# Zeros for the idle fill, an early exponential, other homes for the words of w_v, and a new order table

## The chip, the cores and the metric

The kernel runs on one core of a Trainium2 chip. The metric is the time of one execution on the device, in microseconds (us); the profile shows one such execution, engine by engine. PE is the matrix engine (TensorE), DVE the vector engine, ACT the scalar engine, POOL GpSimd, SP the engine that issues most of the transfers.

## The reference

Three stages on 4 x 576 tokens of width 512: attention with a window of 64 keys, a gated feed-forward block, and a convolution gate with two products. Cut to what is computed:

```python
scores = matmul(q, k.T) / sqrt(64)                      # 4 batches, 8 heads, 576 x 576
mask = (rel >= 0) & (rel < 64)                          # rel = query position - key position
attn = softmax(where(mask, scores, -1e9))
x = matmul(attn, v)                                     # -> 4 x 576 x 512
x_prev = x shifted by one token (zeros at the start)
xk = mu_k * x + (1 - mu_k) * x_prev;  xr = mu_r * x + (1 - mu_r) * x_prev
h = relu(xk @ w_k) ** 2                                 # 512 -> 1024
x = sigmoid(xr @ w_r) * (h @ w_v)                       # r and v, each 512 wide
gate = sigmoid(sum over 5 taps of conv_w[t] * x shifted by t)
out = (gate * (x @ w_val)) @ w_out
```

q, k, v are float32, the weights arrive as 64-bit numbers.

## The kernel before

The 2304 tokens are cut in five blocks: block 0 with 256 tokens, blocks 1 to 4 with 512. For each block there are four attention units, one for each pair of heads, numbered 0 to 19, so that units 0 to 3 belong to block 0 and units 4 to 7 to block 1. A unit is a chain over the engines: `ldqk` and `ldv` (SP issues the loads of q, k and v), `qk` (scores on PE), `top` (row maximum on DVE), `exp` (ACT), `eps`, `rec`, `norm` (the division, DVE), `tp0` and `tp` (transposes of the two heads on PE), `pt` (copies out of PSUM), `pv` (PE), `x` (copy into `xT`). A block's `mix` steps then form xk and xr (`a` on ACT or DVE, `xm` on DVE).

Every weight piece takes a chain of its own. `ld` loads the 64-bit words, `g` (ACT) and `t`, `s` (DVE) make float32 "words" of them, and `hi` and `lo` split these in two fp32r tiles, so that blocks 1 to 4 multiply hi*hi + hi*lo + lo*hi. Activations are split likewise (`xhi`, `xlo`). Block 0 starts earlier: its products `r`, `h` and `v` use the float32 words themselves (line 577), the later blocks the split tiles (line 554). Block 1 cannot start before its `xlo` are written, and these lie in the tile `x` (tag "x"), which before the change is the same memory as the tile `words`. `wide_x` is the step that hands it over: it waits until all ten pieces have given up their words. After block 4 the last stage runs (`val`, `out`), in which POOL issues six accumulating transfers into `gate`.

What runs when is not decided on the chip. Every step has a number in the table SLOT; the steps are sorted by it, and each engine runs its instructions in that order. A step that waits holds everything behind it on its engine, the transfers that SP and ACT issue among them. The costs in `Plan` decide one thing in the program: how many idle passes `fill` puts ahead of a PE step that would wait (line 994). These are products of the identity tile into a spare PSUM tile, meant to keep PE active. Exponentials and sigmoids lie in different tables of ACT; an ACT_TABLE_LOAD stands where they alternate.

Of the kernel before, what the change touches and what calls it, by code (L numbers as in the profile page):

```python
# [8 lines left out]
F32 = mybir.dt.float32  # L9
# [11 lines left out]
P = 128  # L21
# [19 lines left out]
    'first': '5',  # L41
    'cap': '6',
    'ident': '10',
    'low': '11',
    'ldmu': '1',
    'ldc': '14',
    'omu': '27',
    'pg': '59',
    'wc0': '89 26 96',
    'wc': '99',  # L50
    'first_x': '4',
    'ldqk': '0 8 7 16 18 40 105 107 164 209 231 247 301 310 338 401 398 425 445 479',
    'ldv': '20 22 44 46 67 102 211 219 250 280 297 312 355 382 427 441 485 483 540 537',
    'qk': '12 15 25 34 42 76 157 201 226 243 285 304 336 347 393 422 440 476 491 502',
    'top': '13 19 31 41 49 123 165 208 249 264 317 331 346 390 413 435 457 487 498 533',
    'exp': '17 23 43 50 64 141 183 215 260 268 319 334 349 405 420 447 461 489 503 553',
    'eps': 'v24 v35 p51 p58 p75 p152 p192 p223 p267 p276 p325 v343 p358 p410 p430 v450 p466 p508 v509 p556',
    'rec': '29 39 55 72 83 163 204 236 271 281 327 351 359 412 434 458 471 510 525 557',
    'norm': '30 45 62 78 97 184 214 241 277 294 328 353 361 417 438 463 472 511 529 560',
    'tp0': '32 53 68 86 106 194 225 246 283 300 335 360 391 421 448 467 490 515 542 573',  # L60
    'pt': 'a38 v48 a56 v63 a74 a77 a91 a94 a117 a169 a213 a212 a229 a235 a251 a257 a286 a291 a302 a306 a341 '
        'a342 a369 v373 a394 v404 a432 a429 v451 a454 a470 a477 v492 a499 a518 v532 a544 v551 v588 a592',
    'tp': '37 60 71 92 130 207 230 255 289 303 337 368 397 424 452 475 494 522 548 589',
    'pv': '52 66 82 98 185 216 239 273 293 308 350 377 407 436 460 478 512 534 564 600',
    'x': 'v54 v69 a85 a101 a193 a228 a252 a284 a298 a333 a364 v384 v418 a443 a473 a482 a520 v538 a586 a624',
    'mask': '237 258 290 322 340 386 408 428 455 480 496 531',
    'edge': '242 262 295 326 345 389 411 433',
    'a': 'a79 v104 a110 a120 a240 a253 a288 a292 v352 v356 v431 a439 v493 a497 v572 a575 v595 a633 a638 a649',
    'xm': '84 111 114 126 261 272 299 311 383 375 459 446 505 501 578 582 620 640 648 652',
    'xlo': '90 115 119 131 282 287 309 318 419 423 488 474 571 568 584 593 636 646 661 677',  # L70
    'carry': '133 132 278 316 385 464 507 585',
    'r': '93 116 109 124 100 125 112 121 313 320 400 409 554 550 558 567 625 631 639 635 716 728 723 736',
    'sig': '127 128 134 137 329 330 414 437 562 566 576 579 641 642 645 647 725 738 739 750',
    'h': '135 142 144 153 139 146 148 155 168 187 177 188 162 182 174 197 339 354 324 332 363 370 381 387 514 '
        '495 504 517 524 530 536 543 602 603 608 605 614 621 618 609 678 686 682 673 695 700 705 710',
    'relu': 'a158 a167 a160 a166 a191 a195 a198 a203 v348 a362 v344 a366 a374 a378 v388 a396 a516 a519 v513 v523 '
        'a539 a546 a545 v549 v604 a606 v610 v611 a619 v627 a622 a623 v694 a697 a687 a690 a711 a712 v713 a717',
    'sbuf': '170 171 199 205',
    'slo': 'a172 a180 v202 a206 371 379 402 406 535 541 561 563 615 617 637 634 708 709 737 726',
    'v': '210 270 218 234 256 265 248 263 449 469 426 453 415 462 442 481 596 598 591 597 574 583 569 580 650 '  # L80
        '662 658 667 653 672 643 657 749 759 776 789 742 766 755 783',
    'x2': '307 314 323 321 484 465 468 506 601 599 590 594 668 675 674 670 788 794 781 790',
    'xhi': 'a275 a279 v305 a315 a416 v392 a486 a456 a570 a565 v581 a587 v626 a644 v651 v671',
    'cut': '259 296 357 444 500 577',
    'shi': '365 372 380 399 521 527 547 552 607 613 628 629 698 699 719 721',
    'sq': 'a367 a376 v395 a403 v526 a528 a559 a555 v612 v616 v630 a632 a701 v702 a729 a724',
    'staging': '3',
    'w_r ld': '9 21',
    'w_r g': '33 61',
    'w_r t': '36 57',  # L90
    'w_r s': '65 70',
    'w_r hi': 'a113 v80',
    'w_r lo': '145 143',
    'w_k ld': '47 28 122 87',
    'w_k g': '95 81 154 151',
    'w_k t': '108 73 147 140',
    'w_k s': '118 88 159 156',
    'w_k hi': 'v138 a103 v173 v181',
    'w_k lo': '150 129 189 217',
    'w_v ld': '149 136 179 190',  # L100
# [949 lines left out]
```

## Time and profile before

| what | value |
| --- | --- |
| median of 3 runs | 435.81 us (435.57 to 435.96) |
| time of the profiled execution | 435.19 us |
| span of the profiled execution | 433.4 us |
| PE busy | 418.4 us, 97% of the span |
| DVE, ACT busy | 319.8 us, 254.9 us |
| PE's share of the chain that ended last | 90% |

The span runs from the first instruction to the last; 1.8 us of the execution lie around it. A row of the timeline gives start, duration, engine, line, operation, output<-inputs, how many instructions were merged into it, and in brackets how long the engine was idle ahead of it and what ended that.

### The profile page before, as it was taken

The page shows a single profiled execution, that of the slowest core. Times are in us where ns is not written, and L with a number is a line of the kernel's source. Part 1 is how long each engine was busy: PE and PEld are TensorE (multiplying, and loading weights), DVE is VectorE, ACT ScalarE, POOL GpSimd, SP SyncE. Part 2 cuts the span into 40 slices and gives each one's busy share as a digit, 9 for nine tenths or more (in the row PEclk, how much of TensorE's full clock was granted, in tenths as well). Part 3 has the DMA queues.
Part 4 walks back from the last instruction along what each step waited for, and adds up shares of the span by engine and source line. Part 5 has one row for each costly group of instructions (what it writes and reads, how often), then busy time and mean ns, then how long its engine had stood idle before and what let it go on. Part 6 is the DMA issues. An engine that isn't in the chain of part 4 may idle for free.

```text
span 433.4 us, 7910 instructions
## 1 busy us (share of the span) xinstructions
PE 418.4 (97%) x3200; PEld 359.9 (83%) x3200; DVE 319.8 (74%) x443; ACT 254.9 (59%) x581; POOL 23.8 (5%) x66
## 2 busy tenths in 40 slices
PE   5799999899999999999999999999999999999996
PEld 4588787788888888888888888888888999999996
DVE  3999999956976884747314581589996999999960
ACT  3989899697498574394102553045442787785431
POOL 1002202000000100001000000000000000010000
PEclk9999999999999999999999999999999999999999
DMA  7997753722315152100110005220224545543112
GB/s 257 405 332 313 274 170 108 250 68 63 109 47 203 48 174 74 51 0 2 48 50 0 2 0 206 98 97 2 97 88 143 194 98 165 163 117 103 56 56 109
DMA packets 16692, 52.44 MB, mean 121 GB/s; under 512 B 1936, under 2 KB 2704, under 8 KB 15120
## 3 DMA queue, kind: packets, MB, share of 16 engines
q1 hardware_dynamic: 14784, 42.10, 28.0%
q0 software_dynamic: 864, 3.54, 4.1%
q10 hardware_dynamic: 1008, 6.30, 3.8%
q8 instruction: 25, 0.41, 0.4%
q14 instruction: 11, 0.09, 0.1%
HBM read 38.95 MB, written 9.44 MB: 112 GB/s over the span
## 4 chain that ended last, share of the span: by engine, by line
PE 90%; DMA 4%; DVE 2%; ACT 2%; POOL 1%; issue 1%; ACTq 0%; POOLq 0%; DVEq 0%
PE h L554 20%; PE v L554 20%; PE out L554 12%; PE r L554 10%; PE at L467 4%; PE qk L393 4%; PE at L455 3%; PE v L577 3%; PE val3m L785 3%; PE val2m L785 3%; PE val1m L785 3%; PE val0m L785 2%; DMA qk<-qk 2%; DMA words<-w_v 2%; PE r L577 2%; PE h L577 2%
## 5 line engine op out<-in xcount | busy, mean ns | idle before, releaser
L554 PE MATMUL h<-x,wk 128*128 128x512 f32 x384 | 91.1, 393 | 0.0
L554 PEld LDWEIGHTS h<-x,wk 128*128 128x128 f32 x384 | 71.1, 188 | 14.9 <-issue 0.2
L554 PE MATMUL v<-sh,wv 128*128 128x512 f32 x256 | 82.0, 393 | 0.0
L554 PEld LDWEIGHTS v<-sh,wv 128*128 128x128 f32 x256 | 48.0, 188 | 10.1 <-issue 0.2
L554 PE MATMUL v<-sl,wv 128*128 128x512 f32 x128 | 49.8, 389 | 0.0
L603 ACT ACTIVATE rk<-h 128x512 f32<-128x512 f32 (+1 forms) x28 | 14.4, 544 | 56.3 <-PE h L554 47.5
L554 PE MATMUL r<-x,wr 128*128 128x512 f32 x192 | 45.3, 392 | 0.0
L554 PEld LDWEIGHTS r<-x,wr 128*128 128x128 f32 x192 | 35.7, 188 | 7.5
L741 DVE SCALAR_TENSOR_TENSOR gate<-xb,wc,gate 128x576 f32<-128x576 f32 x52 | 40.4, 813 | 0.1
L437 ACT ACTIVATE s<-s,m 128x128 f32<-128x128 f32 x96 | 37.2, 389 | 4.2 <-DVE m L426 4.1
L654 DVE TENSOR_TENSOR sgs<-v,sgs 128x512 f32<-128x512 f32 (+1 forms) x20 | 12.5, 633 | 24.2 <-PE v L554 24.2
L554 PEld LDWEIGHTS v<-sl,wv 128*128 128x128 f32 x128 | 24.1, 188 | 4.7
L460 ACT ACTIVATE pt<-at 128x512 f32<-128x512 f32 (+1 forms) x31 | 16.8, 562 | 18.0 <-PE at L455 17.9
L554 PE MATMUL out<-g0h,wr 128*128 128x288 f32 x128 | 27.0, 295 | 0.0
L554 PE MATMUL out<-g1h,wr 128*128 128x288 f32 x128 | 27.0, 295 | 0.0
L467 PEld LDWEIGHTS at<-pt,vt 128*64 128x64 f32 x576 | 19.4, 140 | 8.3 <-issue 3.3
L455 PE MATMUL at<-ident,s 128*128 128x128 f32 x144 | 23.0, 279 | 2.6 <-DVE s L447 1.5
L467 PE MATMUL at<-pt,vt 128*64 128x64 f32 x576 | 22.5, 228 | 2.0 <-ACT pt L460 0.8
L605 DVE TENSOR_SCALAR rk<-h 128x512 f32<-128x512 f32 x12 | 8.2, 687 | 22.0 <-PE h L554 21.9
L455 PEld LDWEIGHTS at<-ident,s 128*128 128x128 f32 x144 | 16.6, 140 | 8.1 <-issue 1.4
L518 DVE SCALAR_TENSOR_TENSOR xm<-xT,omu,xm 128x512 f32<-128x512 f32 x32 | 22.4, 742 | 0.7 <-POOL xT L524 0.7
L632 DVE TENSOR_TENSOR sl<-rk,sh 128x1024 fp32r<-128x1024 f32 x16 | 19.4, 1221 | 4.7 <-ACT rk L630 4.6
(139 smaller groups left out, 810.6 us busy)
## 6 DMA issues: line engine op xcount, KB each, us to landing
qk<-qk SPq DMA_DIRECT2D x16, 544.0 KB, 4.3
vt<-vh SPq DMA_DIRECT2D x16, 512.0 KB, 4.6
xb<-x2d SPq DMA_DIRECT2D x4, 1152.0 KB, 6.8
out_t<-st SPq DMA_DIRECT2D x15, 288.0 KB, 2.1
x2d<-sgs SPq DMA_DIRECT2D x16, 256.0 KB, 2.0
gate<-tt POOLq DMA_DIRECT2D x6, 576.0 KB, 5.0
words<-w_r SPq DMA_DIRECT2D x2, 1024.0 KB, 7.1
words<-w_k ACTq DMA_DIRECT2D x2, 1024.0 KB, 7.9
```

Source lines behind the costliest of these rows:

```text
L393: PE.matmul(a["ps"][heads[c % 2], h, c // 2 * P:c // 2 * P + P], lhsT=a["q"][heads[h], c * W:(c + 1) * W], rhs=a["k"][heads[h], c * W:c * ...
L437: ACT.activation(out=s, in_=scores()[:, c // n2, c % n2, :] if by_pe else s, func=AF.Exp, scale=D ** -0.5 if by_pe else 1.0, bias=l(0)[:, ...
L455: PE.transpose(a["tp", h][:, c * P:(c + 1) * P], a["s"][:, h * n2 + c, :], ident)
L460: ("act", p_ns(n), lambda h=h: ACT.activation(out=a["pt"][:, h, :n], in_=a["tp", h][:, :n], func=AF.Copy)),
L467: PE.matmul(a["o"][heads[h], c * W:(c + 1) * W], lhsT=a["v"][:, c, heads[h]], rhs=a["pt"][:, h, c * W:(c + 1) * W], start=True, stop=True)
L518: V.scalar_tensor_tensor(out=m, in0=xT[:, f, :n], scalar=omu[:, c:c + 1], in1=m, op0=ALU.mult, op1=ALU.add)
L554: PE.matmul(ps, lhsT=a, rhs=b[:, kt, :], start=(kt == 0 and i == 0), stop=(kt == nk - 1 and i == 2))
L577: PE.matmul(Ps[key][:, :n], lhsT=ws(kt), rhs=x()[:, kt, :], start=kt == 0, stop=kt == nk - 1)
L603: ACT.activation(out=o, in_=ps, func=AF.Relu)
L632: lambda E: E.tensor_tensor(out=Ss[t][1][:, f, :n], in0=rk(), in1=f32(Ss[t][0][:, f, :n]), op=ALU.subtract))
L741: V.scalar_tensor_tensor(out=g, in0=src, scalar=c, in1=g, op0=ALU.mult, op1=ALU.add)
L785: PE.matmul(z[bank][:, j, :HS], lhsT=lhs, rhs=rhs, start=new and kt == 0 and e == 0, stop=kt == 1 and e == 2, skip_group_check=not new)
```

## The change

Six things are changed.

- **Fill.** The idle passes of PE read a tile of zeros, `warm`, the first 128 columns of `sgs`, which POOL writes as its first own instruction. They no longer need the identity.
- **An exponential of one column.** A new step `table` runs one on ACT, into the first column of the second quarter of `sgs`.
- **DMA scratch.** The scratch for POOL's transfers is 2048 bytes per partition.
- **Words of w_v.** The space that this frees holds a new tile `early` (three pieces of 1024 words). The words of w_v lie there and in the second half of `rk`; those of w_r and w_k stay in `words`. `wide_x` waits for six pieces instead of ten, and for two `s`. In block 1 the odd pairs of `relu` wait for `lo` of w_v's last piece and for one `v` of block 0.
- **Loads** of the later pieces are issued from ACT, once the `s` of an earlier piece is done (before: its `hi`).
- **Costs and SLOT** are new.

```diff
 SLOT = {
-    'first': '5',
-    'cap': '6',
+    'first': '33',
+    'cap': '5',
+    'warm': '2',
+    'table': '462',
...
-    START, LAND = 700, 1100
-    RAMP, SLOW = 3500, 1.6
-    WAIT, PASS = 700, 480
+    BEGIN, START, LAND = 740, 700, 1270
+    RAMP, STALL = 3500, 1300
+    WAIT, PASS = 700, 600
...
+    early = const.tile([P, 3 * 1024], F32, name="early")
...
+    warm = sgs[:, 0, :P]
+    op("warm", "pool", 110, [], lambda: G.memset(warm, 0.0))
+    op("table", "act", 100, ["warm"], lambda: ACT.activation(out=sgs[:, 1, :1], in_=warm[:, :1], func=AF.Exp), table="exp")
...
+        E = ACT if queue == "act" else DMA
+        op((key, "ld"), queue, 60 if queue == "act" else 420, [*after, *([(prev, "s")] if prev else [])],
+           lambda: E.dma_start(out=raw_of(), in_=w_dram[key[1]].bitcast(I32)), moves=2.55 * n)
...
-                    Rk[t, p] = rks[:, p % 2]
+                    Rk[t, p] = rks[:, p % 2] if t else rks[:, 0, :, p % 2 * TA:(p % 2 + 1) * TA]
...
-            plan.any(("relu", t, 2 * p + i), [("h", t, 2 * p + i), *back("slo", 2), *([("relu", t, 2 * p)] if i else [])],
+            plan.any(("relu", t, 2 * p + i), [("h", t, 2 * p + i), *back("slo", 2), *([("relu", t, 2 * p)] if i else []),
+                      *([(("w_v", 3), "lo"), ("v", 0, 3)] if t == 1 and p % 2 else [])],
...
-        Q["raw"] = [a.bitcast(I32) for a in (w[:, 0], w[:, 1], xr[:, 1], sr[:, 1])]
-        Q["sw"] = [w[:, 2 + i, j * 1024:(j + 1) * 1024] for i in range(2) for j in range(2)]
+        Q["raw"] = [a.bitcast(I32) for a in (xr[:, 1], sr[:, 1], w[:, 0], w[:, 1])]
+        s = [w[:, 2 + i, j * 1024:(j + 1) * 1024] for i in range(2) for j in range(2)]
+        Q["sw"] = s + s[:2] + [early[:, j * 1024:(j + 1) * 1024] for j in range(3)] + [rks[:, 1].rearrange("p i n -> p (i n)")]
...
-    op("wide_x", "none", 0, [(p[0], "lo") for p in pieces] + [u for p in pieces for u in users[p[0]]], wide_x)
+    op("wide_x", "none", 0, [(p[0], "lo") for p in pieces[:6]] + [u for p in pieces[:6] for u in users[p[0]]]
+       + [(p[0], "s") for p in pieces[6:8]], wide_x)
...
-            PE.matmul(idle["ps"][:, 0, :P], lhsT=ident, rhs=ident, start=True, stop=True)
+            PE.matmul(idle["ps"][:, 0, :P], lhsT=warm, rhs=warm, start=True, stop=True)
...
-    nc = bacc.Bacc("TRN2", target_bir_lowering=False, num_devices=1)
+    nc = bacc.Bacc("TRN2", target_bir_lowering=False, num_devices=1, dynamic_dma_scratch_size=2048)
```

What the new table does to the order is shown at three places. The first is the queue of SP near the program's start, before the change; the names qk, vt, w_r and w_k are those of the tiles and weights, and the qk rows with 1088 columns belong to units 4 and 5.

```order
L323 DMA words<-w_r 128x2048
L288 DMA cw<-conv 128x40
L366 DMA qk_133<-qk 128x576
L366 DMA qk_189<-qk 128x1088
L372 DMA vt_193<-vh 128x512
L323 DMA words<-w_r 128x2048
L372 DMA vt_193<-vh 128x512
L323 DMA s_117<-w_k 128x2048
L366 DMA qk_255<-qk 128x1088
```

The same place of the same queue after the change.

```order
L329 DMA s_114<-w_r 128x2048
L372 DMA qk_184<-qk 128x1088
L378 DMA vt_188<-vh 128x512 x2
L329 DMA x_113<-w_r 128x2048
L372 DMA qk_261<-qk 128x1088
L378 DMA vt_286<-vh 128x512 x2
L329 DMA words<-w_k 128x2048 x2
L372 DMA qk_311<-qk 128x1088
```

Unit 5's load, the second row with 1088 columns, moved from behind the first piece of w_k to ahead of it, and `conv` is gone from here. Once w_r's `s` is done, ACT issues the third piece of w_k beside this queue.

The second place is DVE ahead of block 1, before the change. L329 is the `lo` of a weight piece, L408 a unit's mask, L426 its `top`, L447 its `norm`, L518 `xm`, and L541 the `xlo` of block 1.

```order
L329 TENSOR_TENSOR wv_77<-words,wv_76 128x8x128
L426 TENSOR_REDUCE m_827<-s_770 128x8
L329 TENSOR_TENSOR wv_77<-words,wv_76 128x8x128
L408 SCALAR_TENSOR_TENSOR s_847<-qk_795,cap 128x1024
L518 SCALAR_TENSOR_TENSOR xm<-xT,omu,xm 128x512 x2
L426 TENSOR_REDUCE m_866<-s_847 128x8
L329 TENSOR_TENSOR wv_77<-words,wv_76 128x8x128 x2
L445 RECIPROCAL m_827<-m_827 128x8
L518 SCALAR_TENSOR_TENSOR xm<-xT,omu,xm 128x512 x2
L447 TENSOR_TENSOR s_770<-s_770,m_827 128x1024
L445 RECIPROCAL m_866<-m_866 128x8
L541 TENSOR_TENSOR x<-xm,x 128x1024 x2
```

DVE ahead of block 1 after the change; L547 is `xlo`, L335 `lo`, L662 the `x2` of block 0.

```order
L547 TENSOR_TENSOR x<-xm,x 128x1024
L313 TENSOR_SCALAR x_113<-x_113 128x1024
L547 TENSOR_TENSOR x<-xm,x 128x1024
L315 SCALAR_TENSOR_TENSOR early<-early,x_113 128x1024
L432 TENSOR_REDUCE m_926<-s_849 128x8
L524 SCALAR_TENSOR_TENSOR xm<-xT,omu,xm 128x512 x2
L545 CAST x<-xm 128x1024
L547 TENSOR_TENSOR x<-xm,x 128x1024
...
L662 TENSOR_TENSOR sgs<-v_0_842,sgs 128x256
L335 TENSOR_TENSOR wv_78<-rk,wv_77 128x8x128
```

The four `lo` of w_v moved from ahead of block 1's `xlo` to behind them. Ahead of the `xlo` that block 1's first product needs DVE now has four `lo`, one mask, one `norm` and one cast less. PE has one attention unit less there (16 rows of `qk`, 8 transposes, 16 rows of `pv`), and block 1 begins with `h` instead of `r`.

The third place is ACT in block 1, where the exponential of the new step (L294) stands; L443 are the exponentials of the units, L466 and L480 copies.

```order
L443 ACTIVATE s_1549,m_1557<-s_1549,m_1557 128x128 x8
L466 ACTIVATE pt_1624<-at_1625 128x512
L480 ACTIVATE xT<-at_1588 128x512
L511 ACTIVATE xm<-xT,sm 128x512 x2
L466 ACTIVATE pt_1624<-at_1656 128x512
L294 ACTIVATE sgs<-sgs 128x1
L480 ACTIVATE xT<-at_1680 128x512
```

It is row 125 of ACT's 281 in this list. The first table load stands where it stood, ahead of unit 0's exponentials, as row 2. The new step writes, at that place, one column of `sgs` in which a sigmoid of block 1 lies until the product with `v` has read it.

At the very start PE has four idle instructions (three before), then `qk` of units 0 and 1 with no fill between them (before: two), then five.

## Rows read from the trace of the kernel before

**Rows 1.** The page: the span.

```profile
span 433.4 us, 7910 instructions
```

**Rows 2.** Windows: busy us, (instructions) of PE, PEld, DVE, ACT, POOL; PEclk, DMA share, GB/s.

```profile
0.00:10.00 10.00, 5.50 (x64) 4.56 (x66) 2.48 (x9) 2.87 (x10) 1.95 (x11) 1.00 0.76 246
10.00:20.00 10.00, 7.29 (x130) 5.01 (x131) 9.86 (x24) 9.91 (x46) 0.57 (x3) 1.00 1.01 400
...
20.00:22.00 2.00, 1.65 (x34) 1.41 (x32) 2.00 (x6) 2.00 (x5) 0.26 (x1) 0.56 1.03 429
...
350.00:400.00 50.00, 50.00 (x377) 50.00 (x377) 48.56 (x69) 36.34 (x55) 4.05 (x6) 1.00 0.49 131
```

**Rows 3.** Timeline of PE, its first instructions.

```profile
3.09 1.65 PE L994 MATMUL idle<-ident 128*128 128x128 f32 x6 [3.09 <-POOL ident masks.py:199]
...
4.90 1.16 PE L393 MATMUL qk<-qk 64*64 64x128 f32 x16
5.99 0.98 PE L994 MATMUL idle<-ident 128*128 128x128 f32 x4
...
7.04 0.65 PE L393 MATMUL qk<-qk 64*64 64x128 f32 x16
```

**Rows 4.** Transfers issued in the first 0.9 us: KB, us to landing.

```profile
qk<-qk SPq DMA_DIRECT2D x1, 288.0 KB, 3.0
```

**Rows 5.** Timeline of POOL, DVE and ACT near the start.

```profile
2.47 0.20 POOL masks.py:197 MEMSET ident<- 128x128 f32 x1
3.07 0.23 DVE L283 CAST one<-ident 128x128 bf16<-128x128 f32 x1 [0.32 <-POOL ident masks.py:199]
7.12 1.28 ACT L437 ACT_TABLE_LOAD   x1 [7.12 <-DVE m L429]
15.81 1.18 ACT L301 ACTIVATE words<-words 128x1024 f32<-128x1024 f32 x1
```

**Rows 6.** The chain that ended last, around unit 5's load: start us, us, what.

```profile
12.36 8.19 DMA qk<-qk
```

**Rows 7.** Timeline of PE from unit 5's scores to block 0's first product.

```profile
19.81 0.41 PE L385 MATMUL qk<-low,one 64*64 64x512 bf16 x4 [0.24 <-ACT s L437]
...
20.59 1.99 PE L393 MATMUL qk<-qk 64*64 64x128 f32 x32 [0.35 <-DMA qk<-qk]
22.51 1.12 PE L467 MATMUL at<-pt,vt 128*64 128x64 f32 x16
23.56 0.99 PE L455 MATMUL at<-ident,s 128*128 128x128 f32 x4
24.39 1.03 PE L577 MATMUL r<-x,words 128*128 128x256 f32 x4
25.35 0.69 PE L467 MATMUL at<-pt,vt 128*64 128x64 f32 x16
```

**Rows 8.** Timeline of PE ahead of block 1.

```profile
74.32 0.63 PE L455 MATMUL at<-ident,s 128*128 128x128 f32 x4 [0.66 <-DVE s L447]
74.88 1.10 PE L393 MATMUL qk<-qk 64*64 64x128 f32 x32
...
77.46 1.15 PE L467 MATMUL at<-pt,vt 128*64 128x64 f32 x30 [0.64 <-ACT pt L460]
79.11 1.06 PE L455 MATMUL at<-ident,s 128*128 128x128 f32 x8 [0.50 <-DVE s L447]
...
82.22 2.11 PE L554 MATMUL r<-x,wr 128*128 128x512 f32 x8
```

**Rows 9.** Timeline of DVE ahead of block 1.

```profile
61.51 1.22 DVE L329 TENSOR_TENSOR wv<-words,wv 128x1024 fp32r<-128x1024 f32 x1
```

**Rows 10.** Tile gate on POOL: duration ns min/median/max, first and last start; issues by line.

```profile
L757 POOL DMA_DIRECT2D gate<-tt x6: 840/844/1017, 344.7 to 387.6; - x6
...
gate<-tt POOLq DMA_DIRECT2D x6, 576.0 KB, 5.0
```

**Rows 11.** Transfers by line: a piece of w_k issued by ACT.

```profile
words<-w_k ACTq DMA_DIRECT2D x2, 1024.0 KB, 7.9
```

More of the change, by code (lines that the diff above doesn't have):

```diff
@@ L194, in run @@
             t = max((end[d] + hop[d] for d in ready), default=0)
-            t = max(t + (self.TO_PE if w[0] == "pe" and t else 0), free.get(w[0], 0) if w[0] != "none" else 0)
+            t = max(t + (self.TO_PE if w[0] == "pe" and t else 0), free.get(w[0], self.BEGIN))
             t += self.TABLE if tab and tab != table else 0
             table = tab or table
-            if w[0] == "pe" and self.fill and t - free.get("pe", 0) > self.WAIT:
-                self.fill(t, int((t - max(free.get("pe", 0), 1500) - 250) // self.PASS))
-            free[w[0]] = end[key] = t + w[1]
+            if w[0] == "pe" and self.fill and t - free.get("pe", self.BEGIN) > self.WAIT:
+                self.fill(t, int((t - max(free.get("pe", 0), 1100) - 250) // self.PASS))
+            end[key] = t + w[1]
+            if w[0] != "none":
+                free[w[0]] = end[key]
             hop[key] = self.HOP[w[0]]
             if moves:
-                link = max(link, end[key] + self.START) + moves * (self.SLOW if link < self.RAMP else 1)
+                new = max(link, end[key] + self.START) + moves
+                link = new + self.STALL * (link < self.RAMP <= new)
                 end[key] = link + self.LAND
@@ L307, in words, with weight @@
                                           op0=ALU.logical_shift_left, op1=ALU.bitwise_or))
[L309 removed]
+    def weight(key, w_dram, dst, nm, raw_of, s_of, prev=None, sprev=None, after=(), free=(), used=(), queue="dma"):
         nk = w_dram.shape[2] // nm
         n = nk * nm
[L316 to L323 removed]
+        raw = lambda: raw_of().rearrange("p (k m t) -> p k m t", k=nk, t=2)
+        s = lambda: s_of().rearrange("p (k m) -> p k m", k=nk)
+        E = ACT if queue == "act" else DMA
+        op((key, "ld"), queue, 60 if queue == "act" else 420, [*after, *([(prev, "s")] if prev else [])],
+           lambda: E.dma_start(out=raw_of(), in_=w_dram[key[1]].bitcast(I32)), moves=2.55 * n)
         words(key, n, raw, s, [(key, "ld")], [*used, *([(sprev, "lo")] if sprev else [])])
@@ L396, in qk @@
                               skip_group_check=by_pe)
-        op(("qk", u), "pe", 1040 * nc_ // 8 + 270 * by_pe, [("ldqk", u), *(["low"] if by_pe else []), *([] if t else ["idle"])], qk,
+        op(("qk", u), "pe", 1034 * nc_ // 8 + (208 if t == 0 else 241) * by_pe, [("ldqk", u), *(["low"] if by_pe else []), *([] if t else ["idle"])], qk,
            ring=("pq" if t else "p0", ("exp" if by_pe else "mask", u)))
@@ L429, in top @@
             V.tensor_scalar(out=l(0), in0=l(0), scalar1=D ** -0.5, scalar2=None, op0=ALU.mult)
-        op(("top", u), "dve", v_ns(n * 2) + 72 * by_pe, [("qk" if by_pe else "edge" if firsts else "mask", u), *back2("norm")], top)
+        op(("top", u), "dve", v_ns(n * 2) + 190 * by_pe, [("qk" if by_pe else "edge" if firsts else "mask", u), *back2("norm")], top)
         def exp():
@@ L456, in unit @@
         for h in range(2):
[L457 removed]
+            op(("tp", u) if h else ("tp0", u), "pe", 88 * n2 + 2, [("norm", u), "ident", *back("pv", 1), *([("tp0", u)] if h else [])], lambda h=h: tp(h),
                ring=("pa", ("pt", u, h)))
```

41 lines of the change are left out of this document (16 added, 25 removed), and 200 rows, old and new, of the table SLOT.

## The prediction

> **What bounds the kernel now.** The page comes first: the span is 433.4 us [rows 1], and by the table above PE is busy for 97% of it and makes nine tenths of the chain that ended last. The order table neither adds nor removes a product, so PE's useful work stays what it is. [...]
>
> The start: PE's first pass comes at 3.09, block 0's first product only at 24.39 [rows 3, 7]. In between, ACT and DVE are busy 9.91 and 9.86 of 10 us [rows 2]: they work through the exponentials and through the weights' words, and PE waits for them. So what starts these two engines earlier is worth its full length, until something else holds PE.
>
> The stretch from 19.8 to 24.4: unit 5's scores wait 0.24 us for an exponential and 0.35 for their own load, whose step in the chain is 8.19 us long [rows 6, 7]. [...]
>
> The stretch ahead of block 1: three waits of 0.66, 0.64 and 0.50 us, two for a `norm` on DVE and one for a copy on ACT [rows 8].
>
> Behind it the trace has no wait of PE until the last stage begins. That stage is PE-bound too, with PE busy for 50 of 50 us and DVE for 48.56 [rows 2].
>
> **The change part by part. The fill and the first scores (A).** Unit 0's load lands 3.0 us after its issue at 0.74, so at 3.75 [rows 4]. Its float32 scores started only at 4.90, because six idle passes, started at 3.09 when the identity was there, lay ahead. They ran until 6.06 at the low clock: 16 rows in 1.16 us, against 0.65 for unit 1 [rows 3]. After the change the fill waits for a memset of the size that takes 0.20 us [rows 5], issued at about 0.74, so I put the first pass at 1.0. Eight passes at 1.65/6 = 0.275 us end at 3.2. The mask operands are ready at 3.07 + 0.23 = 3.30 [rows 5], the load at 3.75, so the float32 part starts at about 3.8. Before, the clock rose between 5.99 (four passes in 0.98 us, still slow) and 7.04 (fast) [rows 3], so 2.9 to 3.95 after the first pass; the same lead from 1.0 gives 3.9 to 4.95. The scores then end between 3.8 + 0.65 = 4.45 and 3.8 + 1.16 = 4.96. I take 4.85, near the slow end, since most of the rise's interval lies behind 4.45. That is 1.2 us sooner than 6.06; bounds 1.1 and 1.6. The maximum, the table load and the exponentials follow as one chain, so all of it is passed on.
>
> **The early exponential (nothing).** The order puts the new step in block 1, as row 125 on ACT, and leaves the first table load ahead of unit 0's exponentials. So the load's 1.28 us [rows 5] stays on the path. The step itself is one column, less than a copy, on an engine with room there; without that cover it would cost one short ACT instruction.
>
> **Unit 5's load and the low clock (B).** In SP's queue one piece of w_k, 1024 KB, no longer lies ahead of unit 5's load. At the 400 GB/s of [rows 2] that is 2.6 us of transfer. The load is still issued when unit 3's scores are done, 1.2 us earlier than 12.36, so it lands at 11.2 + 8.2 - 2.6 = 16.8 instead of 20.55. Unit 4's exponentials, which free the score tile, ended just ahead of the 0.24 us wait's end at 19.81 [rows 7], say at 19.6. One pass over a weight piece, 1.18 us [rows 5], has gone behind them, so they end near 19.6 - 1.2 - 1.2 = 17.2, and PE finds the data there. What it lost here is 0.24 + 0.35 of waits, and at the low clock 1.99 - 1.10 for the scores, 1.12 - 0.69 for `pv`, 0.99 - 0.53 for the transposes [rows 7, 8]: together 2.4 us. The waits should go. Whether the clock falls again I can't tell: PE is hardly denser in that time than before. If it falls while PE waits it costs nothing, if it falls under the products it costs up to the 1.8 as before. I take 1.5 for B; bounds 0 and 2.4.
>
> **Words of w_v out of block 1's x (C).** The three waits ahead of block 1 come to 1.8 us [rows 8]. DVE had four `lo` of w_v ahead of block 1's `xlo`, because `wide_x` needed them, each 1.22 us [rows 9]. After the change these four, one mask and one `norm` (1024 columns as well, so I put them at 1.2 us each) stand behind: 7.3 us less ahead. With A, DVE can deliver 8.5 us sooner. PE asks for it sooner by A + B = 2.7, by the 1.8, and by the one unit that moved behind (1.10 + 1.06 + 1.15 = 3.3 us [rows 8]): 7.8 in all. DVE delivers in time, with 0.7 us to spare. So I count 1.8 for C; bounds 0 and 1.8. The cover is thin: if DVE falls behind by more than that, this gain is what goes.
>
> **New waits (D).** Unit 6's scores now stand between block 0's first four products and the rest, and their load lies in SP's queue behind two pieces of w_k. By the shapes in that queue, 4 x 288 + 3 x 544 + 4 x 256 + 4 x 1024 KB, 8.1 MB, have to move until it has landed; 2.5 are through by 10 us (246 GB/s), the rest at 400 GB/s [rows 2] by 24. PE reaches it at about the same time. Unit 7's scores need unit 6's exponentials, since there is one score tile. I charge 0.8 us for both; bounds 0 and 3.0, the upper one being a whole set of eight exponentials, as the one row that PE would wait for.
>
> **No cost.** The smaller scratch, which no row shows at work: POOL issues six transfers between 344.7 and 387.6 us, one in 8.6 us, and one has landed 5.0 us after its issue [rows 10]. If the scratch held only one, an issue would wait where two come closer than 5 us, and DVE's taps behind it; that is between 0 and 5 us, and I take 0, since on average the one before is long through. `conv`'s load moves far behind, but its words are first needed in the last stage. The new wait of `relu` in block 1: `lo` of w_v's last piece stands some seven 1.2 us passes and smaller ones behind the `xlo` that lets block 1 start. PE has three `h` tiles and a unit to do before it needs a bank that this `relu` frees, over 10 us.
>
> **The sum.** - 1.2 (A) - 1.5 (B) - 1.8 (C) + 0.8 (D) = - 3.7. The profiled execution took 435.19, span and the 1.8 around it, and becomes 431.5. The median of the runs lies 0.6 above it: 435.8 - 3.7 = 432.1 us. With every bound at its better end the gain is 5.8 (430.0), with the clock and the new waits at their worse end 1.1 - 0 + 1.8 - 3.0, no gain (435.9).
>
> **The rivals.**
>
> *The low clock moves onto block 0's products.* The granted clock fell after ten microseconds of sparse work [rows 2], and PE stays as sparse up to its first products, which come some 3 us sooner. [...] For it speaks that nothing fills those gaps; against it, that the two shortest gaps go. [...] Chance 0.17.
>
> *Transfers interleave and unit 6 is late.* ACT issues the third piece of w_k some 7 us before unit 6's load is through, beside SP's queue. If the two queues share the transfer engines evenly, 1024 KB at 400 GB/s put up to 2.6 us ahead of unit 6's load. PE waits, D is 3.4 instead of 0.8, and the time 434.7. A piece on ACT's queue took 7.9 us to land [rows 11], three times its own 2.6, so it does share. [...] Chance 0.13.
>
> *The last stage stalls: slower.* It is ordered anew as well, and DVE has only 1.44 us in 50 to spare [rows 2] while PE waits for nothing. A DVE pass put one place too late for a `val` or `out` product lets PE wait 0.8 to 1.2 us. There are four sequences; if the loss passes 3.7 + 0.9, so about five such waits, the kernel is slower. At six it is 432.1 + 6 = 438. Against it: the last products of block 4, their stores and the copy that frees `val` stand in the same order as before. Chance 0.07.
>
> *The start is bound by DVE anyway.* If the words of the weights and not unit 5 set when block 0 gets going, B and A shrink to A's 1.1, C stays and D is paid: 433.7. Chance 0.13.
>
> **How the numbers follow.** My forecast has 0.5, the four rivals 0.5. About 0.2% (0.9 us) is what a measurement of this kernel can tell from no change. Faster: the forecast, and most of the first, second and fourth, 0.86. Within 0.2%: the tails of those, 0.06. Slower: the third and a combination of the first two, 0.08. The range goes down to the sum of the better ends and up over the first, second and fourth rivals and what they cost a little more than worked out; it leaves out the third: 429.9 to 435.2.
>
> **What would show it.** A: first fill at 1.0, unit 0's scores over before 5, the first table load still there, at 5.9 instead of 7.12. B: unit 5's load landing at about 17, no wait for it on PE, no granted clock near 0.56 under products. C: no wait between block 0's last `v` and block 1's first `h`, at about 75 us. D: PE waits for a load or exponential between 24 and 34. The forecast is wrong if block 1 begins later than 79 us (82.2 [rows 8] less the moved unit), or if PE waits inside the last stage.

## The result, and the profile after

The changed kernel takes 431.02 us (median of 4 runs, 430.81 to 431.66) against 435.88 us (4 runs, 435.57 to 436.50) for the kernel before on the same chip: a ratio of 0.989, 95% interval 0.987 to 0.991. It is faster by 4.9 us in the medians and by 4.0 us between the two profiled executions (431.17 after 435.19). The forecast of 432.1 lies 1.1 us above the median, which is inside the range.

The step `table` ran at 141.1 us. Block 1's sigmoids had been written to `sgs` by then (106.7 to 120.6) and were read only later (148.8 to 154.1), so one column of one of them is replaced. The times are those of the kernel as it stands; in the experiments that put `table` at the start this does not happen.

The page of the changed kernel, its span and the busy times of the engines (against [rows 1] and the table of the profile before):

```profile
span 429.4 us, 7914 instructions
...
PE 416.0 (97%) x3202; PEld 358.9 (84%) x3202; DVE 321.9 (75%) x445; ACT 251.5 (59%) x579; POOL 19.7 (5%) x66
```

The same windows as in [rows 2], with the same columns:

```profile
0.00:10.00 10.00, 7.11 (x85) 5.97 (x85) 3.80 (x13) 4.09 (x18) 2.05 (x11) 1.00 0.81 290
10.00:20.00 10.00, 7.95 (x159) 5.68 (x160) 9.81 (x23) 9.74 (x42) 2.08 (x5) 1.00 1.02 406
20.00:22.00 2.00, 1.73 (x10) 1.36 (x11) 1.97 (x3) 0.58 (x2) 0.00 (x0) 1.00 1.06 438
350.00:400.00 50.00, 50.00 (x377) 50.00 (x376) 49.03 (x71) 36.06 (x54) 4.01 (x6) 1.00 0.51 131
```

In this execution the granted clock (third number from the end) does not fall at 20 us, where it stood at 0.56 before. The last stage is still PE's, 50 of 50 us. In the first 10 us the transfers move 290 GB/s instead of 246.

The timeline of PE and ACT at the start (against [rows 3] and the table load of [rows 5]):

```profile
0.99 2.08 PE L1004 MATMUL idle<-sgs 128*128 128x128 f32 x8 [0.99 <-POOL sgs L293]
...
3.72 1.13 PE L399 MATMUL qk<-qk 64*64 64x128 f32 x16
...
4.85 1.16 PE L399 MATMUL qk<-qk 64*64 64x128 f32 x16
...
5.89 1.28 ACT L443 ACT_TABLE_LOAD   x1 [5.89 <-DVE m L435]
```

The idle passes start 2.1 us sooner and no longer stand in front of unit 0's scores, which start at 3.72 instead of 4.90. These scores still run at the low level (16 rows in 1.13 us), and so do those of unit 1 (1.16). This is read from the durations, since the same 16 rows take 0.65 us later; the windows print a granted clock of 1.00 here all the same. The table load comes 1.23 us sooner.

PE's timeline from there to block 0's `h` (against [rows 7]):

```profile
20.91 2.76 PE L583 MATMUL r<-x,words 128*128 128x256 f32 x12
...
26.03 0.41 PE L391 MATMUL qk<-low,one 64*64 64x512 bf16 x4 [0.25 <-ACT s L443]
...
27.45 1.10 PE L399 MATMUL qk<-qk 64*64 64x128 f32 x32 [0.98 <-DMA qk<-qk]
...
37.09 0.66 PE L461 MATMUL at<-ident,s 128*128 128x128 f32 x4 [1.36 <-ACT xT L480]
```

Block 0's first product comes 3.48 us sooner than the 24.39 of [rows 7]. Then three new waits, 0.25 + 0.98 + 1.36 = 2.6 us, take most of that back. The chain that ended last shows what stands behind two of them (start us, us, what):

```profile
13.54 13.86 DMA qk<-qk
...
27.45 1.15 PE qk L399 x32
...
31.91 1.59 DVE x L524 x4
...
33.64 2.79 POOL xT L553
...
36.45 0.61 ACT xT L480
...
37.09 0.66 PE at L461 x4
```

It runs from the load of unit 6 (13.86 us to landing) over DVE to a copy on POOL of 2.79 us, the step `carry`, and from there to the transposes that PE waits for. Between the load's landing and the copy into `xT`, ACT is not in it.

Ahead of block 1, DVE's last `xlo` and PE's first `h` (against [rows 8, 9]):

```profile
73.16 1.23 DVE L547 TENSOR_TENSOR x<-xm,x 128x1024 fp32r<-128x1024 f32 x1
...
75.74 3.09 PE L560 MATMUL h<-x,wk 128*128 128x512 f32 x12
```

PE has no wait between 37.6 and here: the three of [rows 8] are gone. 82.22 less the 3.3 us of the moved unit would be 78.92, so about 3.2 us are gained by block 1. The first `val` starts at 327.2 instead of 331.4: 4.2 us, so 1.0 more came from the blocks between. In the last stage 0.2 went again, since the first wait of `val` is 0.9 us instead of 0.6. The sum is the 4.0 us between the two spans.

### The profile page after: what moved, and what is told of

Same layout as the page of the kernel before. It is cut to its first block, busy times and chain, and to the rows that moved or that the text cites. A ratio compares the mean times of both kernels' runs of the same rounds, so it can differ in the third digit from the quotient of the medians.

```text
span 429.4 us, 7914 instructions
## 1 busy us (share of the span) xinstructions
PE 416.0 (97%) x3202; PEld 358.9 (84%) x3202; DVE 321.9 (75%) x445; ACT 251.5 (59%) x579; POOL 19.7 (5%) x66
## 4 chain that ended last, share of the span: by engine, by line
PE 88%; DMA 4%; DVE 3%; ACT 2%; POOL 1%; issue 1%; ACTq 0%; POOLq 0%; DVEq 0%; SPq 0%
PE h L560 20%; PE v L560 19%; PE out L560 12%; PE r L560 10%; PE at L473 4%; PE at L461 3%; PE qk L399 3%; PE v L583 3%; DMA qk<-qk 3%; PE h L583 3%; PE val3m L793 3%; PE val2m L793 3%; PE val1m L793 3%; PE val0m L793 2%; ACT s L443 1%; DMA st<-w_out 1%
## 5 line engine op out<-in xcount | busy, mean ns | idle before, releaser
L610 ACT ACTIVATE rk<-h 128x512 f32<-128x512 f32 (+1 forms) x29 | 14.7, 544 | 47.4 <-PE h L560 37.4
L443 ACT ACTIVATE s<-s,m 128x128 f32<-128x128 f32 x96 | 37.2, 393 | 6.1 <-DVE m L432 6.1
L662 DVE TENSOR_TENSOR sgs<-v,sgs 128x512 f32<-128x512 f32 (+1 forms) x20 | 12.3, 630 | 19.0 <-PE v L560 19.0
L637 DVE TENSOR_TENSOR rk<-rk 128x1024 f32<-128x1024 f32 x9 | 11.0, 1221 | 18.5 <-ACT sh L634 18.5
L547 DVE TENSOR_TENSOR x<-xm,x 128x1024 fp32r<-128x1024 f32 x16 | 19.4, 1215 | 7.0 <-ACT x L544 6.9
L473 PE MATMUL at<-pt,vt 128*64 128x64 f32 x576 | 21.5, 225 | 1.2 <-DVE pt L467 0.9
L634 ACT ACTIVATE sh<-rk 128x1024 fp32r<-128x1024 f32 x16 | 16.8, 1059 | 9.9 <-DVE rk L612 9.8
```

What stands on the lines that cost most here:

```text
L443: ACT.activation(out=s, in_=scores()[:, c // n2, c % n2, :] if by_pe else s, func=AF.Exp, scale=D ** -0.5 if by_pe else 1.0, bias=l(0)[:, ...
L473: PE.matmul(a["o"][heads[h], c * W:(c + 1) * W], lhsT=a["v"][:, c, heads[h]], rhs=a["pt"][:, h, c * W:(c + 1) * W], start=True, stop=True)
L547: lambda E: E.tensor_tensor(out=dst(1), in0=src(), in1=f32(dst(0)), op=ALU.subtract))
L610: ACT.activation(out=o, in_=ps, func=AF.Relu)
L634: ACT.activation(out=Ss[t][0][:, f, :n], in_=rk(), func=AF.Square)
```

## The experiments

Every kernel but one is an edit of the changed kernel. In the profiles of most of them the granted clock fell to 0.5 to 0.6 somewhere between 16 and 22 us, so each is read by where block 1's first `h` stands as well as by its time. The kernel before had medians of 435.5 to 436.3 in these comparisons.

**The changed kernel again** (no edit).

> The changed kernel once more, nothing altered. In its first profile the granted clock stays at full level from 4 to 32 us; in the profiles of two kernels that have the same instructions up to 25 us or further (carry on DVE, lo ahead) it fell to 0.5 to 0.6 between 16 and 21 us, and block 0's first product came at 21.85 instead of 20.91. Theory 1 (the fall is a matter of the single execution, not of the order): the time scatters by some 0.5 us between executions, this profile shows a first product at either 20.9 or 21.9, and if it is 21.9, PE's wait of 0.98 for unit 6's load shrinks by as much and block 1's first h stands at 75.7 to 75.9 all the same. Rival (each order has its clock): first product at 20.9 again, no fall.

431.47 us (6 runs, 431.16 to 432.42; ratio 0.990, 0.988 to 0.992). Windows of PE and all engines (columns as above), and PE's timeline:

```profile
18.00:20.00 2.00, 2.00 (x37) 1.78 (x38) 1.73 (x5) 2.00 (x5) 0.32 (x1) 0.51 1.05 444
20.00:22.00 2.00, 1.90 (x28) 1.21 (x20) 1.44 (x3) 0.69 (x2) 0.00 (x0) 0.64 0.99 414
```

```profile
18.53 1.95 PE L399 MATMUL qk<-qk 64*64 64x128 f32 x30
...
22.29 2.76 PE L583 MATMUL r<-x,words 128*128 128x256 f32 x12
...
27.39 1.10 PE L399 MATMUL qk<-qk 64*64 64x128 f32 x32
...
75.69 3.10 PE L560 MATMUL h<-x,wk 128*128 128x512 f32 x12
```

The same program, and this time the clock fell under unit 5's scores (30 rows in 1.95 us, 1.07 in the first profile). Block 0's first product is 1.4 us later, and yet unit 6's scores start at 27.39, now without a wait, and block 1 at 75.69. Theory 1 holds: the same program runs with the fall and without it, and in this order it costs nothing, because unit 6's load lands at 27.4 either way. The first four runs say the same: the one with the lowest mean clock (0.996) was the shortest, 430.81, and the longest, 431.66, had 1.000.

**A later load of w_k's fourth piece.**

```diff
-    'w_k ld': '49 46 108 71',
+    'w_k ld': '49 46 108 97',
```

> The load of the fourth piece of w_k on ACT's queue gets number 97 instead of 71, so it is issued at about 26 us, not at 15.9, and no longer moves beside unit 6's load. Theory 1 (the two queues share the transfer engines, the second rival of the prediction): unit 6's load lands up to 2.6 us sooner, at about 25 instead of 27.4, and PE's wait of 0.98 us for it goes. Rival (it lands at 27.4 whatever stands on ACT's queue, since SP's own queue has the bytes ahead of it): the wait stays. Even under theory 1 the next thing is close: the products of r need DVE's xm, which end at 28.5 in the changed kernel, so that I expect no more than 0.4 us at block 1's first h.

432.31 us (4 runs, 430.19 to 432.69; ratio 0.991, 0.988 to 0.994). The transfers that SP issues at 13.5 us, first in the changed kernel, then here (KB, us to landing):

```profile
qk<-qk SPq DMA_DIRECT2D x1, 544.0 KB, 13.9
```

```profile
qk<-qk SPq DMA_DIRECT2D x1, 544.0 KB, 11.2
```

In `SLOT` the piece is the fourth of w_k; in time it is the third to be issued, the one that the prediction speaks of. Unit 6's load lands 2.7 us sooner, and PE's wait for it is gone: theory 1's mechanism holds, the two queues do share. The time did not follow, since PE came to those scores only at 27.7. One reason is a fall of the clock between 18 and 22 (0.59 and 0.56 in the two windows); another stands ahead of it in PE's timeline:

```profile
18.28 0.66 PE L461 MATMUL at<-ident,s 128*128 128x128 f32 x2 [1.01 <-ACT pt L466]
```

In the changed kernel these transposes waited 0.43 us, for a copy on DVE, and ran at 17.66. The wait for ACT, 0.83 to 1.02 us, is in the profiles of all three kernels with the later load and in neither of the changed kernel, so it seems to come with the edit; why is open. The time also goes with the clock, as far as four runs can tell: the run with a mean clock of 0.998 took 430.19, the three with 0.990 to 0.996 took 432.16 to 432.69.

**The table load at the start.**

```diff
-    'table': '462',
-    'ldmu': '3',
+    'table': '2',
+    'ldmu': '1',
...
+        n = (idle.setdefault('n', [5, 4]) or [0]).pop()
```

> The early exponential is put where nothing waits for it: step `table` gets number 2 (with `ldmu` at 1 ahead of it), and the idle passes are held at the 8 and 10 of the changed kernel. The table load then stands at about 1.0 us instead of 5.89, and unit 0's exponentials start 1.28 us sooner. Theory 1 (ACT and DVE set the pace of the start, so whatever starts them earlier is passed on, as in term A of the prediction): block 0's first product at 19.6 instead of 20.91, block 1's first h about 1.2 us sooner (74.5), the whole 1.2 us faster. Theory 2 (transfers set it: unit 6's load lands at 27.4 because of the bytes ahead of it, whatever ACT does): the load lands between 27.0 and 27.4 again, PE's wait for it grows from 0.98 to about 2 us, and at most 0.4 us is left at block 1. I hold theory 2 the likelier.

431.96 us (4 runs, 431.64 to 433.87; ratio 0.992, 0.990 to 0.995). PE's timeline in the profiled execution, the longest of the four:

```profile
20.07 2.75 PE L583 MATMUL r<-x,words 128*128 128x256 f32 x12
...
26.40 0.41 PE L391 MATMUL qk<-low,one 64*64 64x512 bf16 x4 [1.46 <-ACT s L443]
...
27.96 1.98 PE L399 MATMUL qk<-qk 64*64 64x128 f32 x32 [1.12 <-DMA qk<-qk]
```

The table load stands at 1.18 and ACT's first exponential at 5.93, 1.26 us sooner. Of this 0.8 arrive at the first product and nothing at unit 6's scores: their load lands at 27.9, half a microsecond later than before, and ACT waits 2.58 us for words of w_k that are still on their way. Theory 2 holds, and the rest is worse than it said: after the long wait the clock fell (0.50 from 28 to 30 us, 0.65 from 30 to 32), and block 1 began at 78.34. The other three runs, 431.64 to 432.13, are no shorter than the changed kernel's medians of 431.0 and 431.5 either, so no gain shows.

**The copy `carry` on DVE.**

```diff
-        op(("carry", t, g), "pool", 90, ...
-           lambda: G.tensor_copy(xT[:, f, 0:1], xT[:, f, n:n + 1]))
+        op(("carry", t, g), "dve", 90, ...
+           lambda: V.tensor_copy(xT[:, f, 0:1], xT[:, f, n:n + 1]))
```

> The step `carry` (a copy of one column for two tiles, 128x2) runs on DVE instead of POOL, at the same number; nothing else changes. In the changed kernel one of these copies takes 2.78 us on POOL and ends at 36.45, and behind it ACT's copy into xT waits 1.38 us and PE's transposes 1.36 us (at 37.09). Theory 1 (the slow copy on POOL makes this wait): the copies take about 0.1 us each on DVE, the transposes come 1.2 to 1.4 us sooner, and block 1's first h too (74.4 to 74.6 instead of 75.74). Rival (the wait goes on for another reason, since ACT still has its table load of 1.28 us and a sigmoid ahead of that copy, or DVE's xlo for block 1 is late by then): less than 0.5 us at block 1.

430.04 us (4 runs, 429.55 to 431.04; ratio 0.987, 0.985 to 0.990). Timeline of DVE and PE:

```profile
34.63 0.23 DVE L553 COPY xT<-xT 128x2 f32<-128x2 f32 x2
...
35.16 1.29 PE L461 MATMUL at<-ident,s 128*128 128x128 f32 x8
...
36.29 4.05 PE L583 MATMUL h<-x,words 128*128 128x256 f32 x18
...
74.44 3.11 PE L560 MATMUL h<-x,wk 128*128 128x512 f32 x12
```

Both copies take 0.23 us, the wait of 1.36 is gone, and block 1 begins 1.30 us sooner, although the clock fell here (0.63 and 0.52 from 16 to 20 us) and the first product came at 21.85. Theory 1 holds. This is the shortest kernel measured; its interval overlaps with those of the changed kernel, so that only the profile, not the ratio, sets it apart.

**The fill: the identity again, and no first fill.**

```diff
-    op("idle", "none", 0, ["warm"], first_idle)
+    op("idle", "none", 0, ["ident"], first_idle)
...
-            PE.matmul(idle["ps"][:, 0, :P], lhsT=warm, rhs=warm, start=True, stop=True)
+            PE.matmul(idle["ps"][:, 0, :P], lhsT=ident, rhs=ident, start=True, stop=True)
```

(with `idle` at number 11; the second kernel instead returns from `fill` while its modelled time is below 4500 ns)

> Term A undone alone: the idle passes read the identity again and wait for it, 8 and 10 passes as in the changed kernel. The first eight should run from about 3.1 to 5.2, unit 0's float32 scores start at 5.3 instead of 3.72, and the first table load stand at 7.4 instead of 5.89. Theory 1 (the prediction: maximum, table load and exponentials follow as one chain, so all of it is passed on): first product about 22.4, block 1's first h 1.5 us later (77.2), kernel 1.5 us slower than the changed one. Rival (unit 6's load lands at 27.4 because of the bytes ahead of it, not because of ACT, so up to 1 us of the delay fits into PE's wait for it): first h at 75.9 to 76.5, 0.2 to 0.7 us slower.

> The eight idle passes ahead of unit 0's scores are left out; the second set of ten stays. Theory 1 (term A's gain is that the passes no longer stand ahead of the scores, and at that place they buy no clock that counts): scores from 3.7 to 4.85 at the low level as with them, table load at 5.89, first product within 0.3 us, kernel the same. Rival (they raise the clock in time for what follows): the clock rises some 2.4 us later, since PE's first work comes at 3.4 instead of 1.0, so the scores of units 2 and 3 run at the low level too (1.16 instead of 0.65 us each), and the first product comes 0.5 to 1 us later.

The identity: 433.60 us (10 runs, 432.94 to 434.95; ratio 0.995, 0.994 to 0.997), 2.1 us above the changed kernel on the same chip. Its PE timeline, and the window from 8 to 10 us of it and then of the changed kernel:

```profile
5.33 1.16 PE L399 MATMUL qk<-qk 64*64 64x128 f32 x16
...
29.89 1.10 PE L399 MATMUL qk<-qk 64*64 64x128 f32 x32 [1.66 <-DMA qk<-qk]
```

```profile
8.00:10.00 2.00, 1.14 (x10) 1.05 (x10) 0.61 (x2) 1.99 (x8) 0.00 (x0) 1.00 0.66 156
```

```profile
8.00:10.00 2.00, 0.81 (x23) 0.60 (x22) 1.21 (x4) 2.00 (x13) 0.00 (x0) 1.00 0.93 359
```

The scores come 1.6 us later, and more than that arrives: the rival is out, since unit 6's load does not stay at 27.4 but lands at 29.9. It is issued 1.6 us later, at 15.12, and takes 14.7 us instead of 13.9. The last two numbers of the windows give one reason. SP issues loads behind scores, the later scores leave the transfer engines a third idle for two microseconds, and 0.4 MB that isn't moved then, 1.0 us at 400 GB/s, is missing later. From 12 to 18 us about as much again is missing, although the engines are busy then (0.96 and 0.97); that is not explained. So here a delay ahead of a full queue was passed on, while time won ahead of it (the table load) was not. The profiled execution, 434.92 us, is one of the longest: its block 1 begins 3.5 us later, at 79.22, with a second wait for a load (0.97 us at 69.25), so the price is better read from the medians.

Without the first fill: 431.73 us (4 runs, 431.03 to 433.77; ratio 0.991, 0.988 to 0.995), the scores at 3.81 for 1.13 us and 4.94 for 1.16, the first product at 20.99. Theory 1: at this place the eight passes buy nothing that the time shows. Block 1 began 0.5 us later, at 76.27: unit 6's scores came 0.3 us later (27.73), and the wait for `xT` was 1.57 us instead of 1.36; why that load landed later is open.

**hi and lo of w_v ahead of block 1's xlo**, first by numbers from 240 to 257, then directly ahead of the last pair (the edit shown).

```diff
-    'w_v hi': 'v325 a285 a292 a287',
-    'w_v lo': '333 405 321 302',
+    'w_v hi': 'v279.1 v279.2 a292 v279.3',
+    'w_v lo': '279.4 279.5 321 279.6',
```

> The order part of term C undone, the tiles left where they are: `hi` and `lo` of three pieces of w_v go back ahead of block 1's xhi and xlo (numbers 240 to 257). That is 3 x 1.22 us of lo and one hi of 0.69 us, 4.35 us on DVE, ahead of the xlo for which block 1's first h waits. Theory 1 (DVE's row ahead of these xlo is what block 1 waits for, and the change freed it): DVE delivers 1.4 us ahead of need in the changed kernel, so PE waits 4.35 - 1.4 = 3 us ahead of block 1, first h at about 78.7, and the kernel is about 3 us slower (434). Rival (DVE has room elsewhere to take it, or h follows PE's own row): under 1 us.

> Term C's order undone more cleanly: `hi` and `lo` of three pieces of w_v, all on DVE, stand directly ahead of the last xhi and xlo that block 1's h needs, and behind every words step that block 0's v needs. That is 3 x 0.60 and 3 x 1.14 us, by the starts of such rows 5.2 us. Theory 1 (DVE's row ahead of this xlo decides when block 1 begins): that xlo ends at 74.4 + 5.2 = 79.6 instead of 74.4, block 1's first h comes at about 79.8 instead of 75.7, with a wait of PE of 4 us there, and the kernel takes about 4 us more (435.5). Rival (PE finds other work or DVE had idle time there): first h before 78, under 2 us slower.

The first: 435.29 us (10 runs, 434.10 to 436.59; ratio 0.999, 0.998 to 1.000). Block 1 began at 79.91, 4.2 us later, but PE's wait of 2.42 us stood elsewhere, in front of the last `v` but one of block 0, whose words I had moved back as well. PE ran slowly behind that wait (32 rows of `pv` in 1.98 us instead of 1.15, a mean granted clock of 0.91 from 60 to 80 us), which makes up the rest. So this one says nothing on the question. The second: 434.95 us (10 runs, 434.53 to 435.91; ratio 0.998, 0.997 to 0.999). Timeline of PE there:

```profile
75.98 1.74 PE L560 MATMUL h<-x,wk 128*128 128x512 f32 x6
78.50 0.50 PE L560 MATMUL h<-x,wk 128*128 128x512 f32 x1 [0.79 <-DVE x L545]
79.76 1.43 PE L560 MATMUL h<-x,wk 128*128 128x512 f32 x5 [0.76 <-DVE x L547]
...
83.32 0.63 PE L461 MATMUL at<-ident,s 128*128 128x128 f32 x4 [1.09 <-DVE s L453]
```

The waits are here now, though not ahead of the first `h`, which comes at 75.98, where I had put the rival. `h` starts with the half of its input that is there, and stops in the middle for the other: 0.79, 0.76, and 1.09 for a `norm` that is late too. The second `h` starts at 83.70 instead of 80.21, 3.5 us later, of the 4 expected, and the time follows. DVE's row ahead of block 1 does decide once it is longer than its 1.4 us of room, in size as theory 1 says.

**Combinations.** The table load, the later load and `carry`; and the last two alone.

> Three edits together: the table load at the start (`table` at number 2), the fourth piece of w_k loaded later on ACT's queue (number 97), `carry` on DVE. Apart, the first lost time since unit 6's load and the words of w_k came no sooner than before, the second made that load land 2.7 us sooner but PE was late at it by a fall of the clock, the third took 1.3 us off. Theory 1 (transfers are what ate the table load's 1.28 us, and with the fourth piece out of the way it gets through): block 1's first h at 73.0 to 73.6 instead of 75.74, kernel near 428.5. Rival (ACT and DVE's own row sets the pace from 24 us on, or the clock falls): first h at 74.4, no better than carry on DVE alone, kernel near 430.

> carry on DVE and the later load of w_k's fourth piece together, the table load left at 5.89. Theory 1 (unit 6's load no longer holds PE, so that a fall of the clock between 16 and 22 us, where it comes, is now seen in the time): without a fall first h near 73.5 and about 429.2 us, with one near 74.4 to 74.9 and 430. Rival (the load's landing was of no weight): no better than carry on DVE alone, 430.0, whatever the clock.

All three: 430.94 us (6 runs, 430.65 to 431.77; ratio 0.989, 0.987 to 0.992); clock at 0.50 to 0.60 from 16 to 22 us, first product only at 23.35, block 1 at 75.19. The two: 430.79 us (4 runs, 430.36 to 431.21; ratio 0.989, 0.988 to 0.991), clock at 0.50 from 20 to 22, block 1 at 74.57. Neither beats `carry` alone. That is what the second's rival says; 74.57 is also what its theory 1 says for an execution with a fall, so the two are not told apart, and the 429.2 us without a fall is not shown. Both kernels have the transposes' wait for ACT near 18.4 us (0.83 and 1.02 us), the same as with the later load alone.

**Five `pv` steps one product earlier.**

```diff
-    'pv': '... 282 328 352 387 414 442 464 484 504 531 567 594',
+    'pv': '... 282 319.5 352 378.5 406.5 434.5 464 484 504 525.5 567 594',
```

> Five `pv` steps (units 9, 11, 12, 13 and 17) are put one product earlier, with the copies `pt` that two of them need, so that a product of twelve rows stands right behind each of them where scores stood before. PE's work is the same. In the chain of the changed kernel a product behind a pv takes 2.95 us, behind transposes 2.77, behind another product 2.72 to 2.74. Theory 1 (it is this that made the stretch from block 1's first h to the first val 1 us shorter than its work before: there twelve products stand behind a pv, in the changed kernel three): five more rows of 2.95, and that stretch takes 252.4 us instead of 251.4. Rival (the 1 us is something else, a wait or the transfers): 251.4 again, within 0.2 us, and no more rows of 2.95 than three.

433.06 us (10 runs, 432.21 to 434.79; ratio 0.993, 0.991 to 0.994). (An earlier version with four steps moved, without the copies, gave no time.) The chain of the changed kernel, a product behind another step, behind transposes and behind a `pv`; then one behind a `pv` here, and one in the kernel before:

```profile
76.09 2.74 PE h L560 x12
...
80.46 2.78 PE h L560 x12
...
161.66 2.95 PE h L560 x12
```

```profile
195.55 2.95 PE v L560 x12
```

```profile
100.34 2.95 PE h L554 x12
```

Seven single rows of 2.93 to 2.95 stand in its chain, where the changed kernel has two. From block 1's first `h` (75.62) to the first `val` (328.4) it takes 252.8 us, against 327.2 - 75.74 = 251.5: 1.3 longer, 1.0 expected. Theory 1 holds.

**The smaller scratch in the kernel before.**

```diff
-    nc = bacc.Bacc("TRN2", target_bir_lowering=False, num_devices=1)
+    nc = bacc.Bacc("TRN2", target_bir_lowering=False, num_devices=1, dynamic_dma_scratch_size=2048)
```

> The kernel before with nothing but the smaller DMA scratch (2048 bytes per partition). The prediction put this at 0, with bounds 0 and 5 us. Theory 1: POOL's six accumulating transfers are issued on average 8.6 us apart and take about 5 us, so none waits for room: the time within 0.2% of the kernel before, and these issues at the same places in the last stage. Rival: the scratch holds only one such transfer, an issue waits where two come closer than 5 us, and the last stage is up to 5 us longer.

436.00 us (12 runs, 434.44 to 437.61) against 435.91: ratio 1.001, 1.000 to 1.002. POOL's six issues lie between 346.6 and 389.5, 42.9 us apart as before, and land after 5.0 us. The scratch costs nothing that these runs show; the interval allows 1.0 us.

## Why the forecast came out near, step by step

**A, 1.2 us: the size right, the way half right.** The table load came 1.23 us sooner. Undone alone, with a start 1.6 us later, A costs 2.1 us in the medians. The clock's lead did not carry over: unit 1's scores were still slow up to 6.0 (16 rows in 1.16 us), later than the 3.9 to 4.95 that I had worked out, and my taking the slow end hid that. And the chain that I named, maximum, table load and exponentials, is not what passes it on: with the table load taken out of that chain nothing came through. What the runs point to instead is that the loads behind the scores are issued sooner and the transfers have no hole; the hole accounts for about half of what went missing.

**B, 1.5 us: in the trace 2.25, in the time not what I thought.** Unit 5's load is issued at 11.19 and lands 5.8 us later, at 17.0 (16.8 forecast), and the two waits there, 0.24 and 0.35 us, are gone. Without a fall of the clock the first product gains 3.48 - 1.23 = 2.25 us, with one (22.29) 0.9. Block 1 does not see the difference (75.74 and 75.69). So what B won beyond the waits went straight into D's waits for unit 6. The first rival, the low clock, did come in most profiles of these kernels (0.50 to 0.56 in the lowest two microseconds), ahead of block 0's products and not under them, and in the changed kernel it cost nothing. The upper end of the range takes in a price of this rival that no run shows. What the runs show of slow products in block 0 is less: with the table load at the start twelve rows of `r` took 3.06 us instead of 2.76, where the granted clock was 0.65; in the first kernel with hi and lo of w_v moved, eight rows of `v` took 2.41 instead of 1.89, behind the wait of 2.42.

**C, 1.8 us: right.** No wait is left ahead of block 1, and DVE's last `xlo` is done 1.4 us ahead of its use (0.7 forecast). Putting three `hi` and three `lo` back, 5.2 us of DVE's time, cost 3.5 us.

**D, 0.8 us: the term that was mis-sized; it is 2.6.** I had unit 6's load landing at 24, when PE would come to it; it landed at 27.4, since w_k's fourth piece on ACT's queue moves beside it, 2.7 us of it. That is the second rival's mechanism with its number for the delay, but not its price: PE waited 0.98 for the load, not 2.6, and 0.25 for unit 5's exponentials just ahead of it. In the second execution, where the clock fell, neither wait was there, since PE came later. The other half, 1.36 us, is a wait that I had not looked for: `carry` on POOL, 2.78 us for 128x2 elements, in front of ACT's copy into `xT`.

**Not in the sum: 1.0 us between block 1 and the last stage.** I had looked for time only where PE waits, fills or runs slowly. But what stands ahead of a product matters too. In the chain of the kernel before, twelve products stand directly behind a `pv` or scores, in that of the changed kernel three, and each such place costs 0.2 us: 1.9 us. Some 0.7 goes back: the moved unit aside, transposes stand directly behind scores eight times there instead of four, where they take 0.59 us instead of 0.44 and the product behind them 0.03 more. That leaves 1.2 us, near the 1.0 measured.

**The sum again.** A, B, C and D as the trace shows them, 1.2 + 2.25 + 1.8 - 2.6, make 2.7 us by block 1, where 3.2 were measured. A fourth wait that is gone (0.19 us for `pt`, at 53.9 in the kernel before) is part of the difference; 0.3 is not attributed. With 1.0 behind block 1 and 0.2 lost in the last stage it is 4.0, against 3.7. That D's 1.8 too few was made up by what B won and by what I had not counted is luck. The forecast's other 0.8 us lies in the step to the median: I had added 0.6 to the profiled execution, and here the median is 0.15 below it.

**At nothing: right.** The scratch, the early exponential (it is late, the table load stays on the path) and the last stage, where PE waits 0.9 and 0.7 us in `val` as against 0.6 and 0.7: the third rival, a stall there, is out. (My sign of being wrong, a wait of PE inside the last stage, was badly put: the kernel before has these waits too.) The fourth, a start bound by DVE, is out too, since unit 6's load sets it.

## What to carry to other kernels

Here one transfer set the pace: ACT's work ahead of it 1.26 us sooner won nothing, while scores 1.6 us later made it land 2.4 us later. So look for the window in which the transfer engines run below their rate. Before pricing a moved step, list every engine between it and the next product, the small copies on POOL too, because a copy of 128x2 elements held PE for 1.36 us. A fall of PE's clock in a sparse stretch differed between two executions of one program here (1.00 and 0.51 from 18 to 20 us); profile it twice before giving it a price.

## What the hardware showed unexpectedly

Six of the eight copies of `carry` take 0.18 to 0.19 us in this trace, but one took 2.78 and one 0.58. POOL's and DVE's rows in the changed kernel (timeline):

```profile
14.28 1.22 DVE L315 SCALAR_TENSOR_TENSOR words<-words,s 128x1024 int32<-128x1024 int32 x1
14.30 1.25 POOL L448 TENSOR_SCALAR m<-m 128x4 f32<-128x4 f32 x1 [1.47 <-ACT s L443]
...
33.41 1.22 DVE L453 TENSOR_TENSOR s<-s,m 128x1024 f32<-128x1024 f32 x1
33.64 2.90 POOL L553 COPY xT<-xT 128x2 f32<-128x2 f32 x2 [7.38 <-DVE x L524]
34.54 0.69 DVE L333 CAST wr<-words 128x1024 fp32r<-128x1024 f32 x1
35.14 1.22 DVE L335 TENSOR_TENSOR wr<-words,wr 128x1024 fp32r<-128x1024 f32 x1
36.28 1.22 DVE L434 TENSOR_REDUCE m<-qk 128x8 f32<-128x1024 f32 x1
...
136.74 0.68 DVE L545 CAST x<-xm 128x1024 fp32r<-128x1024 f32 x1
136.88 0.58 POOL L553 COPY xT<-xT 128x2 f32<-128x2 f32 x1 [5.38 <-DVE xm L524]
```

The slow copy ends at 36.42, when three DVE instructions on SBUF are through (33.41 to 36.36) and one that reads PSUM begins (36.28); `eps` at 14.30, 0.19 to 0.20 us in most places, takes 1.25 beside one DVE instruction of 1.22 us with two inputs in SBUF; the copy at 136.88 ends with a cast (137.46 and 137.42). Beside a mask, which reads PSUM and one input in SBUF, a copy at 63.40 took 0.19. On DVE the same copies took 0.23 us together. That POOL was held by DVE in these rows is my reading of where they end; it was not isolated.

The clock differs between executions of one program, in its rise as in its fall: from 18 to 20 us it stood at 1.00 in one profile of the changed kernel and at 0.51 in the other, and unit 1's scores ran in 1.16 us in most profiles and in 0.65 in one (the later load) whose instructions are the same up to there. I had put the clock into B as if the order decided it. It may still shift the odds: in three of the changed kernel's ten runs the mean clock is 0.999 or 1.000, in none of the 66 runs of the kernel before beside the experiments is it above 0.996.
